# Spectral filter and state-space mix: the time transform's real and imaginary parts on two halves of the partitions, and the filter's sums inside the inverse matmuls

## The chip, the cores and the metric

The kernel runs on one core of a Trainium2 chip. The metric is the device time of one launch in microseconds (us). Before the change it is 349.39 us, the median of three runs (348.5 to 349.62).

## What is computed

The input x has 2048 time steps of 1024 channels. Two branches read it, and a gate mixes them row by row.

```python
g = sigmoid((x * gate_w).sum(-1, keepdims=True))

X = rfft2(x)                        # over time (2048) and channels (1024 -> 513)
a = irfft2(X * (w_r + 1j * w_i))    # the spectral branch, w of 2048 x 513

Lam_bar = exp(exp(log_dt) * (Lambda_re + 1j * Lambda_im))
Bu = x @ (((Lam_bar - 1) / Lam)[:, None] * (B_re + 1j * B_im)).T
h[t] = Lam_bar * h[t - 1] + Bu[t]   # the state-space branch, 1024 complex states
b = 2 * (h @ (C_re + 1j * C_im).T).real + x * Dskip

out = g * a + (1 - g) * b
```

## The kernel before

Everything is bf16 in SBUF and fp32 in PSUM. The kernel body records operations, each with an engine, a key and an assumed duration; the class Plan (L99 to L221) then orders them, engine by engine: among the operations that its own clock holds ready first, the one with the lowest key goes next. The order on every engine, SyncE's (SP's) queue of DMA issues included, is thus fixed before the launch, and a queue waits at its head. The constants K_... (L820 to L836) set the keys.

**State-space branch.** The 1024 states are eight blocks (jb), each done in two turns of 1024 time steps. `bu` multiplies x by B (64 matmuls a block, L743), ScalarE copies the sums out (L746), VectorE rotates them by a cosine and sine table (`rot`, L711 to L717), scans them (L755) and rotates them back (`rot_out`). Three buffers u hold turns between the matmuls and the scans. `load_BT` (L727) brings B by a transposing DMA on SP, two for a block; `load_CT` (L695) brings C in eight transposing DMAs, each behind a step of the last spectral stage.

**Spectral branch.** The time index of 2048 is split in 128 times 16. The stages are:

- `fd` (L511) and `s1` (L526), 16 steps j: the channel transform, then the 128-point time transform as a complex product, four matmuls of 512 columns (L530 to L533) with the tables T2 and TK. The result, real and imaginary parts side by side in the columns, goes to DRAM (L538).
- `s2w` (L618), 16 steps b, which starts when all of `s1` is in DRAM: it loads a tile Bb across (L620), and the 16 rows b of w_r and w_i (L622, L623, 128 KB each) into the tile wA. Four matmuls with block diagonal cosines and sines (L627 to L630) do the second step of the time transform. ScalarE copies out X2 (L633). VectorE makes the complex product with w: two multiplications of 1024 columns, by w_r and by w_i with the halves swapped (L637, L638), and a difference and a sum of 512 columns (L639, L640), the result X3 in wB. wA has two places for w, wB four for X3.
- The channels 0 and 512 share a column and need a repair: `fixup` (L585) turns that column through DRAM, and GpSimd computes it (L603 to L612) into Qb; ScalarE puts it into column 0 of each X3 (L641).
- `is1` (L643): the 128-point inverse, again four matmuls (L648 to L651), the copy C1 (L654), and a store to DRAM (L655).
- `is2` (L660) and `idft` (L677), 16 steps bp, which start when all of `is1` is in DRAM: a load Cq (L662), 8 small matmuls, a copy ZT (L673), the inverse channel transform, the gate (L690) and a store to DRAM (L691). After the even steps a `load_CT` follows.

**Output.** `yout` (L779), 16 tiles of 128 rows, each 32 matmuls of 512 columns with C (L787), eight small ones for Dskip (L794) and VectorE's sums with the loaded spectral part. Its first tile waits for `idft` step 13, all others for step 15 (the item "step", L790).

**Memory.** Large tiles take one of four places of 16 KB a partition (group "b8") in the order in which they are declared: bn, T2_sb, TK_sb, wA, wB, then the four CT. Bb, X2 and C1 lie in the upper half of the last state buffer; the scans of the blocks 6 and 7 wait until the last of them is read (the item "lodged", L759).

Of the kernel before, what the change touches and what calls it, by code (L numbers as in the profile page):

```python
# [11 lines left out]
ACT = mybir.ActivationFunctionType  # L12
# [23 lines left out]
def _host_consts():  # L36
# [14 lines left out]
    for par in range(2):  # L51
# [19 lines left out]
    c4 = np.kron(np.cos(2 * np.pi * (np.outer(np.arange(16), np.arange(16)) % 16) / 16), np.eye(4))  # L71
    s4 = np.kron(np.sin(2 * np.pi * (np.outer(np.arange(16), np.arange(16)) % 16) / 16), np.eye(4))
    R4 = np.block([[c4, s4], [-s4, c4]])
# [8 lines left out]
        T2=bf(np.stack([Tc, Ts], axis=2)),  # L82
        TK=bf(np.concatenate([-Ts, np.stack([Kc, Ks, -Ks, J, P0], axis=1)], axis=1)),
        R4=bf(R4),
# [144 lines left out]
def kernel(  # L229
# [27 lines left out]
    turn2_dram = dram.tile([2, 16, P, K], BF16, name="turn2_scratch")  # L257
# [57 lines left out]
    vec8 = cpool.tile([8, 5, P], BF16, name="vec8")  # L315
    for i, src in enumerate((B_Lambda_re, B_Lambda_im, B_log_dt, gate_w, B_Dskip)):
        dma(0, 0.05, lambda i=i, src=src: nc.scalar.dma_start(out=vec8[:, i, :], in_=src.rearrange("(j p) -> j p", p=P)),
            w=[("vec8", i)], eng="ACT", issue=0.33)
# [12 lines left out]
    T2_sb = tile_of([P, 16, 2, P], BF16, "T2_sb", "b8")  # L331
    TK_sb = tile_of([P, 21, P], BF16, "TK_sb", "b8")
    R4_sb = cpool.tile([P, P], BF16, name="R4_sb")
    dma(16.1, 2.6, lambda: nc.sync.dma_start(out=G_all, in_=cst["G"].rearrange("p d k -> p (d k)")), w=[("G",)])
    dma(16.2, 2.6, lambda: nc.sync.dma_start(out=T2_sb.t, in_=cst["T2"]), w=[(T2_sb,)])
    dma(16.3, 1.7, lambda: nc.sync.dma_start(out=TK_sb.t, in_=cst["TK"]), w=[(TK_sb,)])
    dma(16.4, 0.2, lambda: nc.sync.dma_start(out=R4_sb, in_=cst["R4"]), w=[("R4",)])
    T2 = lambda j, c: T2_sb.t[:, j, c, :]
    Tn = lambda j: TK_sb.t[:, j, :]
    Kc, Ks, Kns, JJ, J0 = [lambda i=i: TK_sb.t[:, 16 + i, :] for i in range(5)]  # L340
# [47 lines left out]
    def f():  # L388
        for i in range(5):
            nc.tensor.transpose(out=vps.t[:, i, :], in_=vec8[:, i, :], identity=ident[0:8, 0:8])  # L390
    pe(0.5, 0.2, f, r=[("vec8", i) for i in range(5)] + [("ident",)], w=[(vps,)])
# [134 lines left out]
    def s1(j, X1, key):  # L526
        psa = psum([P, 2, K], "ps_s1")

        def f():
            mm(psa.t[:, 0, :], lhsT=T2(j, 0), rhs=X1.t[:, 0, :], start=True, stop=False)  # L530
            mm(psa.t[:, 0, :], lhsT=T2(j, 1), rhs=X1.t[:, 1, :], start=False, stop=True)
            mm(psa.t[:, 1, :], lhsT=T2(j, 0), rhs=X1.t[:, 1, :], start=True, stop=False)
            mm(psa.t[:, 1, :], lhsT=Tn(j), rhs=X1.t[:, 0, :], start=False, stop=True)  # L533
        pe(key, 4 * U, f, r=[(X1,), (T2_sb,), (TK_sb,)], w=[(psa,)])
        A1 = tile_of([P, 2, K], BF16, "A1", "A1")
        act(key, 1.01, lambda: nc.scalar.copy(out=A1.t, in_=psa.t), r=[(psa,)], w=[(A1,)])  # L536
        act(key, 0.2, lambda: nc.scalar.copy(out=Acol[:, j, :], in_=A1.t[:, :, 0]), r=[(A1,)], w=[("Acol", j)])
        dma(key, 0.68, lambda: nc.sync.dma_start(out=turn1_dram[j], in_=A1.t), r=[(A1,)], w=[("t1", j)])  # L538

    Wr_v = A_w_r.rearrange("(p b) k -> p b k", b=16)  # L540
    Wi_v = A_w_i.rearrange("(p b) k -> p b k", b=16)
    Wc, Wc_f, Wh, alpha, beta = [fx.tile([P, 16, n], d, name=m) for n, d, m in (
        (4, BF16, "Wc"), (4, FP32, "Wc_f"), (4, FP32, "Wh"), (2, FP32, "alpha"), (2, FP32, "beta"))]
    Wrev, Zrev = fx.tile([P, 16, 4], FP32, name="Wrev"), fx.tile([P, 16, 2], FP32, name="Zrev")
    Bcol, Qb, Zp = [fx.tile([P, 16, 2], BF16, name=m) for m in ("Bcol", "Qb", "Zp")]
    Zp_f, t1, t2, t3, t4 = [fx.tile([P, 16, 2], FP32, name=m) for m in ("Zp_f", "q1", "q2", "q3", "q4")]
    al2, be2 = [fx.tile([P, 16, 2, 2], FP32, name=m) for m in ("al2", "be2")]
# [8 lines left out]
    def reverse_m(src, ncol, name, dst, item, ditem, key):  # L556
        rps = psum([P, 16, ncol], name + "_ps")

        def f():
            for b in range(16):  # L560
                if b == 0:
                    mm(rps.t[:, 0, :], lhsT=J0(), rhs=src[:, 0, :], start=True, stop=True)
                else:
                    mm(rps.t[:, b, :], lhsT=JJ(), rhs=src[:, 16 - b, :], start=True, stop=True)
        pe(key, 1.0, f, r=item + [(TK_sb,)], w=[(rps,)])
# [19 lines left out]
    def fixup(key):  # L585
# [3 lines left out]
        def f():  # L589
            with nc.allow_non_contiguous_dma(reason="tiny corner turn"):  # L590
                nc.sync.dma_start(out=Bcol, in_=col0_dram.rearrange("(a b) j c -> j a b c", a=8))
        dma(key, 0.6, f, r=[("col0",)], w=[("Bcol",)])
        zps = psum([P, 2, 16], "zps")

        def f():
            mm(zps.t[:, 0, :], lhsT=Kc(), rhs=Bcol[:, :, 0], start=True, stop=False)
            mm(zps.t[:, 0, :], lhsT=Ks(), rhs=Bcol[:, :, 1], start=False, stop=True)
            mm(zps.t[:, 1, :], lhsT=Kc(), rhs=Bcol[:, :, 1], start=True, stop=False)
            mm(zps.t[:, 1, :], lhsT=Kns(), rhs=Bcol[:, :, 0], start=False, stop=True)
        pe(key, 0.5, f, r=[("Bcol",), (TK_sb,)], w=[(zps,)])  # L600
# [5 lines left out]
        pool(key, 0.8, lambda: G_.tensor_mul(out=t1, in0=Zp_f, in1=al2[:, :, 0, :]), r=[("Zp_f",)] + fa, w=[("t1",)])  # L606
        pool(key, 0.8, lambda: G_.tensor_mul(out=t2, in0=Zp_f[:, :, ::-1], in1=al2[:, :, 1, :]), r=[("Zp_f",)] + fa, w=[("t2",)])
        gp(lambda: G_.tensor_add(out=t1, in0=t1, in1=t2), ["t1", "t2"], ["t1"])
        pool(key, 0.8, lambda: G_.tensor_mul(out=t3, in0=Zrev, in1=be2[:, :, 0, :]), r=[("Zrev",)] + fb, w=[("t3",)])
        pool(key, 0.8, lambda: G_.tensor_mul(out=t4, in0=Zrev[:, :, ::-1], in1=be2[:, :, 1, :]), r=[("Zrev",)] + fb, w=[("t4",)])  # L610
        gp(lambda: G_.tensor_add(out=t3, in0=t3, in1=t4), ["t3", "t4"], ["t3"])
        gp(lambda: G_.tensor_add(out=Qb, in0=t1, in1=t3), ["t1", "t3"], ["Qb"])  # L612

    t1_v = turn1_dram.rearrange("j (a b) c k -> b (j a) c k", a=8)
    wA = tile_of([P, 4, 2, K], BF16, "wA", "b8")
    wB = tile_of([P, 4, 2, K], BF16, "wB", "b8")

    def s2w(b, key):  # L618
        Bb = tile_of([P, 2, K], BF16, "Bb", "Bb")
        dma(key - 6, 0.84, lambda: nc.sync.dma_start(out=Bb.t, in_=t1_v[b]), r=[("t1", j) for j in range(16)], w=[(Bb,)])  # L620
        wr, w1, w2 = (wA, "W", b % 2), (wA, "a"), (wA, "b")
        dma(key - 6, 0.43, lambda: nc.sync.dma_start(out=wA.t[:, b % 2, 0, :], in_=Wr_v[:, b, 0:K]), w=[wr + (0,)])  # L622
        dma(key - 6, 0.43, lambda: nc.sync.dma_start(out=wA.t[:, b % 2, 1, :], in_=Wi_v[:, b, 0:K]), w=[wr + (1,)])  # L623
        ps2 = psum([P, 2, K], "ps_s2")

        def f():
            mm(ps2.t[:, 0, :], lhsT=Kc(), rhs=Bb.t[:, 0, :], start=True, stop=False)  # L627
            mm(ps2.t[:, 0, :], lhsT=Ks(), rhs=Bb.t[:, 1, :], start=False, stop=True)
            mm(ps2.t[:, 1, :], lhsT=Kc(), rhs=Bb.t[:, 1, :], start=True, stop=False)
            mm(ps2.t[:, 1, :], lhsT=Kns(), rhs=Bb.t[:, 0, :], start=False, stop=True)  # L630
        pe(key, 4 * U, f, r=[(Bb,), (TK_sb,)], w=[(ps2,)])
        X2 = tile_of([P, 2, K], BF16, "X2", "X2")
        act(key, 1.01, lambda: nc.scalar.copy(out=X2.t, in_=ps2.t), r=[(ps2,)], w=[(X2,)])  # L633
        Wb = lambda i: wA.t[:, b % 2, i:i + 1, :].to_broadcast([P, 2, K])
        wa, wb, X3 = lambda: wA.t[:, 2], lambda: wA.t[:, 3], lambda: wB.t[:, b % 4]
        x3 = (wB, b % 4)
        dve(key, 0.69, lambda: nc.vector.tensor_mul(out=wa(), in0=X2.t, in1=Wb(0)), r=[(X2,), wr + (0,)], w=[w1])  # L637
        dve(key, 0.69, lambda: nc.vector.tensor_mul(out=wb(), in0=X2.t[:, ::-1, :], in1=Wb(1)), r=[(X2,), wr + (1,)], w=[w2])  # L638
        dve(key, 0.42, lambda: nc.vector.tensor_sub(out=X3()[:, 0, :], in0=wa()[:, 0, :], in1=wb()[:, 0, :]), r=[w1, w2], w=[x3 + (0,)])  # L639
        dve(key, 0.42, lambda: nc.vector.tensor_add(out=X3()[:, 1, :], in0=wa()[:, 1, :], in1=wb()[:, 1, :]), r=[w1, w2], w=[x3 + (1,)])  # L640
        act(key + 1, 0.2, lambda: nc.scalar.copy(out=X3()[:, :, 0], in_=Qb[:, b, :]), r=[("Qb",)], w=[x3 + (0,), x3 + (1,)])  # L641

    def is1(b, key):  # L643
        X3, x3 = lambda c: wB.t[:, b % 4, c, :], (wB, b % 4)
        psc = psum([P, 2, K], "ps_is1")

        def f():
            mm(psc.t[:, 0, :], lhsT=T2(b, 0), rhs=X3(0), start=True, stop=False)  # L648
            mm(psc.t[:, 0, :], lhsT=Tn(b), rhs=X3(1), start=False, stop=True)
            mm(psc.t[:, 1, :], lhsT=T2(b, 0), rhs=X3(1), start=True, stop=False)  # L650
            mm(psc.t[:, 1, :], lhsT=T2(b, 1), rhs=X3(0), start=False, stop=True)  # L651
        pe(key, 4 * U, f, r=[x3 + (0,), x3 + (1,), (T2_sb,), (TK_sb,)], w=[(psc,)])
        C1 = tile_of([P, 2, K], BF16, "C1", "C1")
        act(key, 1.01, lambda: nc.scalar.copy(out=C1.t, in_=psc.t), r=[(psc,)], w=[(C1,)])  # L654
        dma(key, 0.86, lambda: nc.sync.dma_start(out=turn2_dram[:, b].rearrange("c u k -> u c k"), in_=C1.t), r=[(C1,)], w=[("t2", b)])  # L655

    t2_v = turn2_dram.rearrange("c b (a g i) k -> i (c b a) g k", a=4, g=2)
    ga_v = ga_dram.rearrange("(p b) n -> p b n", b=16)

    def is2(bp, key):  # L660
# [4 lines left out]
        def f():  # L665
            for kc in range(4):
                par, half = divmod(kc, 2)
                for gg in range(2):
                    mm(psz.t[:, kc, gg, :], lhsT=Cq.t[:, gg, 256 * half + par:256 * (half + 1):2],
                       rhs=R4_sb, start=True, stop=True)  # L670
        pe(key, 0.65, f, r=[(Cq,), ("R4",)], w=[(psz,)])
# [153 lines left out]
    K_TAB = 3.38  # L825
    K_F0 = 21.64
    K_F = 1.92
    K_W0 = 56.28
    K_W = 1.73
    K_WI = 1.83  # L830
    K_I0 = 14.79
    K_I = 8.12
# [91 lines left out]
```

## Time and profile before

The profiled execution has a span of 348.1 us, the median of the plain runs is 349.39 us; the rest lies around the span.

| part of the span (us) | what runs, besides `bu`, its scans and rotations | PE | DVE | ACT |
|---|---|---|---|---|
| 0 to 28 | x loaded and transposed, its halves | 85% | 66% | 72% |
| 28 to 103 | `fd`, `s1` | 99% | 97% | 96% |
| 103 to 124 | the turn through DRAM, first `s2w`, the repair of column 0 | 88% | 97% | 71% |
| 124 to 164 | `s2w`, `is1` | 98% | 96% | 76% |
| 164 to 178 | last `is1`, the turn through DRAM | 99% | 100% | 70% |
| 178 to 228 | `is2`, `idft`, loads of C | 98% | 100% | 91% |
| 228 to 344 | `yout` | 99% | 76% | 1% |

The shares are busy time over the length of the part. Over the whole span PE (TensorE's matmuls) is busy for 333.3 us, DVE (VectorE) for 303.4, ACT (ScalarE) for 193.6 and POOL (GpSimd) for 21.0. A busy share is a mean; what sets the time of a stage is to be read from what it waits for, and from what has no room left in it. The profile counts a matmul of 512 columns as 379 ns, but successive ones start 0.216 us apart.

### The profile page before, as it was taken

What the parts mean: (1) busy time and instruction counts of PE and PEld (TensorE: products, weight loads), DVE (VectorE), ACT (ScalarE), POOL (GpSimd) and SP (SyncE); (2) the same over time, 40 slices, a digit from 0 to 9 for tenths busy, and PEclk for the clock granted to TensorE, in tenths of its full rate; (3) what the DMA queues carried; (4) which work ended last, traced back from release to release, by engine and by line L of the source; (5) the groups of instructions that cost most, each with busy time, mean ns of one, the idle gap of its engine ahead of it and who ended that gap; (6) DMA issues with size and microseconds to landing.
All of it is one profiled execution on the core that took longest, in us unless ns stands there. A gap on an engine that the chain in (4) does not pass through costs nothing. (4 is left out here: it accounts for less than half of the span.)

```text
span 348.1 us, 5201 instructions
## 1 busy us (share of the span) xinstructions
PE 333.3 (96%) x1909; PEld 175.9 (51%) x1945; DVE 303.4 (87%) x508; ACT 193.6 (56%) x269; POOL 21.0 (6%) x47
## 2 busy tenths in 40 slices
PE   5999999999998999999999999999999999999994
PEld 4655554555543444444447566554544544544442
DVE  2969999899999998999999999999999999942321
ACT  3897999999996776876689999720000000000000
POOL 1180000000004700000000000000000000000000
PEclk9999999999999999999999999999999999999999
DMA  7999310431165789879279999952122222300001
GB/s 246 314 324 123 108 61 32 93 87 66 60 167 109 241 170 322 235 165 222 73 185 229 253 280 258 239 194 83 60 93 99 82 62 90 119 33 30 33 35 55
DMA packets 64433, 49.89 MB, mean 143 GB/s; under 512 B 38932, under 2 KB 51476, under 8 KB 64152
## 3 DMA queue, kind: packets, MB, share of 16 engines
q1 hardware_dynamic: 64136, 49.53, 53.5%
q8 instruction: 15, 0.25, 0.3%
q0 software_dynamic: 192, 0.02, 0.3%
q14 instruction: 10, 0.08, 0.1%
q10 hardware_dynamic: 80, 0.01, 0.0%
HBM read 24.89 MB, written 16.79 MB: 120 GB/s over the span
## 5 line engine op out<-in xcount | busy, mean ns | idle before, releaser
L743 PE MATMUL psu<-xT,BTs 128*128 128x512 bf16 x496 | 115.8, 379 | 1.2 <-DVE xT L365 0.2
L787 PE MATMUL ps_y<-CT,h 128*128 128x512 bf16 x499 | 111.9, 379 | 0.7
L743 PEld LDWEIGHTS <-BTs 128*128 128x128 bf16 x512 | 49.6, 98 | 57.0 <-issue 0.5
L787 PEld LDWEIGHTS <-h 128*128 128x128 bf16 x512 | 49.4, 98 | 56.4 <-DVE h L715 0.2
L755 DVE TENSOR_TENSOR_SCAN h<-r_sb,carry,u 128x512 bf16<-128x512 f32 x48 | 59.6, 1272 | 0.1
L814 DVE SCALAR_TENSOR_TENSOR o<-ps_y,omg,ga 128x1024 bf16<-128x1024 f32 (+1 forms) x17 | 21.0, 1240 | 27.5 <-PE ps_y L794 27.5
L746 ACT CAST u<-psu 128x1024 bf16<-128x1024 f32 x32 | 32.3, 1020 | 12.1 <-PE psu L743 11.9
L517 PE MATMUL ps_fd<-G_all,xpm 128*128 128x512 bf16 x125 | 29.9, 379 | 0.7 <-ACT A L536 0.5
L517 PEld LDWEIGHTS <-xpm 128*128 128x128 bf16 x128 | 18.5, 145 | 10.5 <-issue 0.8
L522 ACT CAST X<-ps_fd 128x1024 bf16<-128x1024 f32 x16 | 21.3, 1334 | 0.1
L711 DVE TENSOR_TENSOR su<-h,pn 128x1024 bf16<-128x1024 bf16 (+1 forms) x24 | 21.1, 878 | 0.1
L712 DVE TENSOR_TENSOR h<-h,pn 128x1024 bf16<-128x1024 bf16 (+1 forms) x24 | 21.0, 876 | 0.1
L711 DVE TENSOR_TENSOR su<-u,cs 128x2048 bf16<-128x2048 bf16 x16 | 19.4, 1215 | 0.3
L712 DVE TENSOR_TENSOR u<-u,cs 128x2048 bf16<-128x2048 bf16 x16 | 19.5, 1220 | 0.1
L755 DVE TENSOR_TENSOR_SCAN h<-r_sb,u 128x512 bf16<-128x512 f32 x16 | 19.2, 1219 | 0.0
L654 ACT CAST h<-ps_is 128x1024 bf16<-128x1024 f32 x16 | 16.2, 1016 | 4.8 <-PE ps_is L651 2.8
L633 ACT CAST h<-ps_s 128x1024 bf16<-128x1024 f32 x16 | 16.1, 1016 | 3.4 <-PE ps_s L630 2.1
L536 ACT CAST A<-ps_s 128x1024 bf16<-128x1024 f32 x16 | 16.5, 1030 | 0.0
L360 PE MATMUL pt<-ident,xn 128*128 128x128 bf16 x128 | 9.9, 242 | 4.0 <-DMA xn<-in_A_x_dram 3.9
L690 ACT ACTIVATE eo<-ps_id,gA 128x1024 bf16<-128x1024 f32 x11 | 12.4, 1168 | 1.9 <-PE ps_id L685 1.9
L673 ACT CAST ZT<-ps_is 128x1024 bf16<-128x1024 f32 x13 | 13.1, 1044 | 0.0
L713 DVE TENSOR_TENSOR h<-h,su 128x512 bf16<-128x512 bf16 (+1 forms) x24 | 12.6, 524 | 0.1
(166 smaller groups left out, 429.1 us busy)
## 6 DMA issues: line engine op xcount, KB each, us to landing
xn<-in_A_x_dram SPq DMA_DIRECT2D x16, 256.0 KB, 5.6
turn_scratch<-A SPq DMA_DIRECT2D x16, 256.0 KB, 2.0
h<-turn_scratch SPq DMA_DIRECT2D x16, 256.0 KB, 3.9
turn_scratch<-h SPq DMA_DIRECT2D x16, 256.0 KB, 4.2
out_dram<-o SPq DMA_DIRECT2D x15, 256.0 KB, 2.2
eoc<-ga_scratch SPq DMA_DIRECT2D x12, 256.0 KB, 2.8
Cq<-turn_scratch SPq DMA_DIRECT2D x11, 256.0 KB, 4.4
ga_scratch<-eo SPq DMA_DIRECT2D x11, 256.0 KB, 2.9
```

Of the source, the lines that this page charges most:

```text
L517: mm(pf.t[:, par].rearrange("p c k -> p (c k)"), lhsT=xA[:, par, db, j, :], rhs=G_sb[:, db, par, :], start=(db == 0), stop=(db == 3))
L522: act(key, 1.3, lambda: nc.scalar.copy(out=X1.t.rearrange("p c (k r) -> p r c k", r=2), in_=pf.t), r=[(pf, 0), (pf, 1)], w=[(X1,)])
L536: act(key, 1.01, lambda: nc.scalar.copy(out=A1.t, in_=psa.t), r=[(psa,)], w=[(A1,)])
L633: act(key, 1.01, lambda: nc.scalar.copy(out=X2.t, in_=ps2.t), r=[(ps2,)], w=[(X2,)])
L654: act(key, 1.01, lambda: nc.scalar.copy(out=C1.t, in_=psc.t), r=[(psc,)], w=[(C1,)])
L711: dve(key, w, lambda: nc.vector.tensor_mul(out=sv(), in0=src()[:, ::-1], in1=bc(1)), r=sitem + [titem(1)], w=[(su,)])
L712: dve(key, w, lambda: nc.vector.tensor_mul(out=dst(), in0=src(), in1=bc(0)), r=sitem + [titem(0)], w=ditem)
L743: mm(psu.t[:, ri, :], lhsT=BT.t[:, ri, db, :], rhs=xT[c][:, db, :], start=(db == 0), stop=(db == 7))
L746: act(kb[cc], 1.01, lambda cc=cc, psu=psu: nc.scalar.copy(out=u.t[:, :, cc, :], in_=psu.t), r=[(psu, 0), (psu, 1)], w=ui(cc))
L755: dve(kd, 1.25, lambda cc=cc, ri=ri, carry=carry: nc.vector.tensor_tensor_scan(out=g()[:, ri, cc, :], data0=rb, data1=u.t[:, ri, cc, :], i ...
L787: mm(psy.t[:, 512 * dh:512 * (dh + 1)], lhsT=hbuf[jb // 4].t[:, jb % 4, ri, P * tb:P * (tb + 1)], rhs=CT[pc].t[:, ri, jb % 2, 512 * dh:512 ...
L814: dve(key - 1, 0.2 + 1.07e-3 * (b - a), lambda a=a, b=b: nc.vector.scalar_tensor_tensor(out=o.t[:, a:b], in0=psy.t[:, a:b], scalar=og, in1 ...
```

## The change

1. **Halves of the partitions.** `s1` now makes, for each parity h of the frequency index, real parts on partitions 0 to 63 and imaginary parts on 64 to 127. It still has four matmuls of 512 columns; their tables are overlapping slices of TF.
2. **Second step in one pass.** `s2w` multiplies the whole tile by one matrix RF: two matmuls for four.
3. **The filter.** X2 is multiplied by w_r and by w_i, each in place over its copy of w (Z(b, 0) and Z(b, 1)). The difference and the sum are gone; `is1` adds the two products in PSUM, with four matmuls as before, whose tables are overlapping slices of MI.
4. **Loads of w.** Both halves of the partitions need the same w, so four DMAs load it (two tensors, two halves, 128 KB each) where two did. wA and wB together now hold w and the products of four steps b; w of step b + 4 is loaded when `is1` of step b has been read.
5. **The repair.** A memset on GpSimd clears column 0 of Z(b, 1). The repaired column goes through four more small matmuls (qps) and a copy (Qz) before ScalarE puts it into Z(b, 0). Its small tensors share memory with others, and GpSimd's first product waits for all eight factors. Bcol is loaded in two DMAs.
6. **Tables.** T2 and TK (1024 and 672 KB) become TF (two tiles of 768 KB) and a small TK. MI (two tiles of 768 KB) is loaded into the places that TF leaves: the second one after the last `s1`.
7. **Keys.** K_TAB, K_W0, K_WI and K_I get other values.

```diff
+    TF_sb = [tile_of([P, 8, 2, 192], BF16, "TF_sb", "b8") for _ in range(2)]
+    TK_sb = cpool.tile([P, 9, P], BF16, name="TK_sb")
+    for i in range(2):
+        dma(16.2, 2.0, lambda i=i: nc.sync.dma_start(out=TF_sb[i].t, in_=cst["TF"][:, 8 * i:8 * (i + 1)]), w=[(TF_sb[i],)])
+    dma(16.3, 1.0, lambda: nc.sync.dma_start(out=TK_sb, in_=cst["TK"]), w=[("TK",)])
...
         def f():
-            mm(psa.t[:, 0, :], lhsT=T2(j, 0), rhs=X1.t[:, 0, :], start=True, stop=False)
-            mm(psa.t[:, 0, :], lhsT=T2(j, 1), rhs=X1.t[:, 1, :], start=False, stop=True)
-            mm(psa.t[:, 1, :], lhsT=T2(j, 0), rhs=X1.t[:, 1, :], start=True, stop=False)
-            mm(psa.t[:, 1, :], lhsT=Tn(j), rhs=X1.t[:, 0, :], start=False, stop=True)
+            tf = TF_sb[j // 8].t
+            for h in range(2):
+                mm(psa.t[:, h, :], lhsT=tf[:, j % 8, h, 64:192], rhs=X1.t[:, 0, :], start=True, stop=False)
+                mm(psa.t[:, h, :], lhsT=tf[:, j % 8, h, 0:128], rhs=X1.t[:, 1, :], start=False, stop=True)
...
+        qps = psum([P, 2, 16], "qps")
+        def f():
+            for odd in range(2):
+                for c in range(2):
+                    mm(qps.t[64 * c:64 * (c + 1), odd, :], lhsT=SEL(odd, c), rhs=Qb[:, :, c], start=True, stop=True)
+        pe(key, 0.3, f, r=[("Qb",), ("TK",)], w=[(qps,)])
+        act(key, 0.2, lambda: nc.scalar.copy(out=Qz, in_=qps.t), r=[(qps,)], w=[("Qz",)])
...
+    MI_sb = [tile_of([P, 16, 192], BF16, "MI_sb", "b8") for _ in range(2)]
+    for i in range(2):
+        dma(30 + 16 * i, 2.0, lambda i=i: nc.sync.dma_start(out=MI_sb[i].t, in_=cst["MI"][:, 16 * i:16 * (i + 1)]), w=[(MI_sb[i],)])
+    home = lambda b: (wA, wB)[b // 2 % 2]
+    Z = lambda b, i: home(b).t[:, 2 * (b % 2) + i]
 
     def s2w(b, key):
         Bb = tile_of([P, 2, K], BF16, "Bb", "Bb")
         dma(key - 6, 0.84, lambda: nc.sync.dma_start(out=Bb.t, in_=t1_v[b]), r=[("t1", j) for j in range(16)], w=[(Bb,)])
-        dma(key - 6, 0.43, lambda: nc.sync.dma_start(out=wA.t[:, b % 2, 0, :], in_=Wr_v[:, b, 0:K]), w=[wr + (0,)])
-        dma(key - 6, 0.43, lambda: nc.sync.dma_start(out=wA.t[:, b % 2, 1, :], in_=Wi_v[:, b, 0:K]), w=[wr + (1,)])
+        wr = (home(b), b % 2)
+        for i in range(2):
+            for c in range(2):
+                dma(key - 6, 0.5, lambda i=i, c=c: nc.sync.dma_start(out=Z(b, i)[64 * c:64 * (c + 1)], in_=W_v[i][b][:, :, 0:K]), w=[wr + (i, c)])
+        pool(key - 4, 0.1, lambda: nc.gpsimd.memset(Z(b, 1)[:, :, 0:1], 0.0), w=[wr + (1, 0), wr + (1, 1)])
...
-            mm(ps2.t[:, 0, :], lhsT=Kc(), rhs=Bb.t[:, 0, :], start=True, stop=False)
-            mm(ps2.t[:, 0, :], lhsT=Ks(), rhs=Bb.t[:, 1, :], start=False, stop=True)
-            mm(ps2.t[:, 1, :], lhsT=Kc(), rhs=Bb.t[:, 1, :], start=True, stop=False)
-            mm(ps2.t[:, 1, :], lhsT=Kns(), rhs=Bb.t[:, 0, :], start=False, stop=True)
+            for h in range(2):
+                mm(ps2.t[:, h, :], lhsT=RF, rhs=Bb.t[:, h, :], start=True, stop=True)
...
-        dve(key, 0.69, lambda: nc.vector.tensor_mul(out=wa(), in0=X2.t, in1=Wb(0)), r=[(X2,), wr + (0,)], w=[w1])
-        dve(key, 0.69, lambda: nc.vector.tensor_mul(out=wb(), in0=X2.t[:, ::-1, :], in1=Wb(1)), r=[(X2,), wr + (1,)], w=[w2])
-        dve(key, 0.42, lambda: nc.vector.tensor_sub(out=X3()[:, 0, :], in0=wa()[:, 0, :], in1=wb()[:, 0, :]), r=[w1, w2], w=[x3 + (0,)])
-        dve(key, 0.42, lambda: nc.vector.tensor_add(out=X3()[:, 1, :], in0=wa()[:, 1, :], in1=wb()[:, 1, :]), r=[w1, w2], w=[x3 + (1,)])
+        for i in range(2):
+            dve(key, 0.69, lambda i=i: nc.vector.tensor_mul(out=Z(b, i), in0=X2.t, in1=Z(b, i)),
+                r=[(X2,)], w=[wr + (i, 0), wr + (i, 1)])
...
     def is1(b, key):
...
+            for h in range(2):
+                at = lambda lo: MI_sb[b // 8].t[:, 2 * (b % 8) + h, lo:lo + P]
+                mm(psc.t[:, h, :], lhsT=at(0), rhs=Z(b, 0)[:, h, :], start=True, stop=False)
+                mm(psc.t[:, h, :], lhsT=at(64), rhs=Z(b, 1)[:, h, :], start=False, stop=True)
...
-    K_TAB = 3.38
+    K_TAB = 4.93
-    K_W0 = 56.28
+    K_W0 = 56.75
-    K_WI = 1.83
+    K_WI = 1.97
-    K_I = 8.12
+    K_I = 10.67
```

## The prediction

> **What bounds the kernel now.** I read the totals first, then the busy time by stage, then the DMAs that two stages issue, then SP's order of issues.
>
> ```profile
> span 348.1 us, 5201 instructions
> PE 333.3 (96%) x1909; PEld 175.9 (51%) x1945; DVE 303.4 (87%) x508; ACT 193.6 (56%) x269; POOL 21.0 (6%) x47
> ```
>
> TensorE is busy for nearly all of the span, and so is VectorE until the last 50 us. By this view alone, work taken from TensorE comes straight off the time. The view by stage has the length, then the busy us of PE, PEld, DVE, ACT and POOL, the clock, the DMA share and GB/s:
>
> ```profile
> 112.00:124.00 12.00, 10.87 (x67) 4.99 (x68) 11.43 (x18) 8.29 (x13) 7.97 (x15) 1.00 0.71 213
> 124.00:164.00 40.00, 39.14 (x178) 17.53 (x180) 38.43 (x69) 30.38 (x44) 0.00 (x0) 1.00 0.91 225
> 164.00:178.00 14.00, 13.89 (x65) 6.34 (x66) 13.98 (x22) 9.75 (x16) 0.00 (x0) 1.00 0.36 114
> 178.00:228.00 50.00, 48.98 (x377) 31.76 (x382) 49.97 (x72) 45.69 (x58) 0.00 (x0) 1.00 1.04 248
> ```
>
> The reader is to see the last column but one. From 124 to 164, where `s2w` and `is1` run, the DMA engines are 0.91 busy, and from 178 to 228 (`is2`, `idft`) 1.04: they have no room left there. So three things are full at once, and the DMAs decide what a change in this stretch is worth. The DMAs issued in these two stages (count, size, median us to landing; the first four rows from 124 to 164, the last two from 178 to 228):
>
> ```profile
> turn_scratch<-h SPq DMA_DIRECT2D x13, 256.0 KB, 4.4
> h<-turn_scratch SPq DMA_DIRECT2D x8, 256.0 KB, 3.9
> wA<-in_A_w_r_dram SPq DMA_DIRECT2D x11, 128.0 KB
> wA<-in_A_w_i_dram SPq DMA_DIRECT2D x11, 128.0 KB, 3.5
> ...
> Cq<-turn_scratch SPq DMA_DIRECT2D x11, 256.0 KB, 4.4
> ga_scratch<-eo SPq DMA_DIRECT2D x9, 256.0 KB, 2.9
> ```
>
> The stages are a chain: `yout` needs `idft` step 15 (L790), `idft` needs all of `is1` in DRAM, `s2w` all of `s1`. From 228 on TensorE runs `yout` back to back (114.95 us busy of 116), so a later start of `yout` is a later end, one for one.
>
> **What one DMA costs.** Two equations, in engine time. From 124 to 164: 0.91 x 40 = 36.4 us for 32 plain loads and stores of 256 KB (13 + 8 + 22 halves) and 4 transposing loads of B of 256 KB. From 178 to 228: 52 us for 29 plain ones (15 Cq, 14 eo) and 17 transposing units (8 loads of C of 512 KB, one of B). They give 0.96 us for a plain 256 KB and 1.42 us for a transposing one. A load of w (128 KB) thus costs 0.48 us.
>
> **The change, part by part.**
>
> TensorE. `s2w` loses 2 of 4 matmuls in 16 steps, 32 in all. In the timeline successive ones of a step start at 124.62, 124.84, 125.05 and 125.27: 0.216 us each, so 6.9 us are gone. `s1` and `is1` keep their 64. The four matmuls of qps are of the kind of L596 to L599, which start 0.03 us apart: nothing.
>
> VectorE. L639 and L640 go: 32 instructions whose mean is 0.422 and 0.428 us, 13.6 us. The two products stay: one of 1024 columns takes 0.682 and 0.688 us with its broadcast or swapped operand (L637, L638), and plain ones of that size take 0.690 (L711, `rot_out`). VectorE is not what ends last after 296, so this only keeps it from being late.
>
> Loads of w. 64 instead of 32, of the same 128 KB. Before, 4 go out at 20 us, 6 from 114 to 123, 22 from 127.85 to 162.2. After, wA and wB hold w for four steps, so 16 go out early, around 20 to 28 us, where the queue is full (0.98 busy from 0 to 28) but the next load on it, of B at 29.37, is for block 2, turns later. The other 48 all wait for `is1` of four steps before; the first `is1` runs at 122.90 now. So the stretch from then on has 48 loads for 22: 48 x 0.48 - 22 x 0.48 = **+12.5 us** of DMA time. No trace row has a load onto half of the partitions. Bounds: 0.37 us, from the best slice of the stage (132 to 134: 370 GB/s at a share of 1.05, so 352 GB/s full), and 0.96, if a load on half the partitions ran at half the rate. The nearest row is the load of w itself, same bytes and same rows of 1 KB, so I take 0.48.
>
> The Trainium skill, page "SBUF — State Buffer", section "Door 1: The DMA port swizzle (why `[64,N]` ≈ `[32,N]`)", says that partitions 0 to 63 reach only 8 of 16 DMA ports, and gives 196 GB/s for them against 328 for all 128. By it a load would be 0.48 x 328 / 196 = 0.80 us (an estimate), and the sum below 21.8 us instead of 6.5. No row of this trace shows it.
>
> SP's queue. The 26 more issues take 0.33 to 0.53 us each, some 11 us, where SP now has issues worth about 23 us in the 40: room, but it waits at its head, and a load of w that waits for `is1` holds the Bb and the stores of C1 behind it.
>
> Tables. MI's second half (768 KB, three units, 2.9 us) goes out at about 103, after the last matmul of `s1`, ahead of the last store of A (issued at 104.3) that the first Bb waits for. From 104 to 108 the engines are 0.35 busy, so 0 to 2.9 us of delay. The repair gets qps and a copy (0.2 us, as L566), up to 1 us before the first `is1`. Together I take **+1 us**, bounds 0 and 3.9. The first half of MI, TF and the small TK move where the share is 0.39 (28 to 103): nothing, and 2.4 us if that room were gone. The memsets on POOL (a MEMSET has 0.10 us) lie between landing and product: hidden while w lands steps ahead, some 0.2 us a step, 3 us in all, if not.
>
> Room that takes it up. From 124 to 164 the engines have 0.09 x 40 = **3.6 us** free. From the last load of w (162.2) to the first Cq (issued at 176.8) 14.6 us pass, of which the chain needs 3.5 (landing) + 1.4 (products) + 0.2 (column) + 0.9 (`is1`) + 1.0 (copy) + 4.2 (store landing) = 11.2; `bu` takes the rest of the slots. So **3.4 us** more.
>
> Sum: 12.5 + 1 - 3.6 - 3.4 = **+6.5 us** for the start of `yout`. The 6.9 us saved on TensorE are then idle time: `bu` runs further ahead in `s2w` (VectorE has 13.6 us more for it) and is missing later, between 178 and 235. The span becomes 354.6 us. The plain median is 1.3 above the profiled span, so **355.9 us**. With a load at 0.37 the sum is 7.2 + 1 - 7 = +1.2 (350.6); at 0.64, a third of the way to the upper bound, it is 30.7 - 10.6 + 1 - 7 = +14.2, so I end this case at 364.
>
> **Rivals.**
>
> *The engines decide (faster).* For it: TensorE has 98% and VectorE 96% in the stretch; the waits named there are small (L637 and L638 waited for w for 0.8 and 0.7 us in all, and ACT 1.6 for a store), so the DMAs only just keep up and do not clearly lead; prefetch four steps deep may fill the queue better than two. Then all of TensorE's 6.9 us come off: 349.39 - 6.9 = 342.5. Against it: the shares of 0.91 and 1.04. If half of the DMA time added is hidden it is some 345.
>
> *It cancels out (same).* `yout` starts at 228 as before, since added traffic just fills the 7 us of room, and the matmuls saved are idle: 349.4.
>
> *Half the partitions, half the rate (much slower).* At 0.96 the 48 loads take 46.1 us: 35.5 + 1 - 7 = +29.5, 379. At 0.72, two loads on opposite halves overlapping partly, 24 + 1 - 7 = +18, 367. For it nothing in this trace; against it, consecutive loads alternate between the halves and can run side by side. The skill's page would have it near 371.
>
> *The loads of w wait for the ring.* Each place is free only after `is1`; its turn is 1.7 (four issues) + 3.5 + 0.2 + 1.4 + 0.2 + 0.9, about 8 us for four steps, against some 16 that the DMAs take. It does not decide, and has its weight in the first case.
>
> **How the numbers follow.** A difference of 0.3%, 1 us, is what a measurement of this kernel tells from none. DMA-paced slower: 0.48. Half rate: 0.10. Same: 0.10. Engines decide: 0.32. The likeliest is 355.9, its own range 350.5 to 364. For 8 in 10 I reach down to 342.5, which takes in most of the faster case, and up to 366, which leaves out most of the half rate. Faster 0.32, same 0.10, slower 0.58.
>
> **What would show it.** Right: DMA share near 1 from about 125 until the first Cq, loads of w landing in over 4 us, the first Cq at about 183 and the first long run of ps_y at about 234 instead of 227.55, with 10 us or more of PE idle before that, and PE still back to back after it; `s2w` with 32 matmuls and DVE near 290 us. Wrong: the first Cq before 177 with PE above 97% from 124 to 228; then the engines set the pace and the time is near 342. Wrong upwards: loads of w that cost over 0.6 us each in a stretch where little else is moved.

## The result, and the profile after

The changed kernel takes 353.17 us (median of 9 runs, 352.50 to 354.36), against 349.69 us (9 runs, 348.5 to 352.5) for the kernel before on the same chip: a ratio of 1.0093, 95% interval 1.0066 to 1.0119. It is slower, by 3.5 us. In this document a time is the median of all executions, while a ratio leaves out those more than 1.5% above the fastest of their kernel (one each of e2, f1, f3, h1 and h2). The profiled span grows from 348.1 to 350.7 us. First the totals of the kernel after, then its busy time by stage (length; busy us of PE, PEld, DVE, ACT, POOL; clock; DMA share; GB/s):

```profile
span 350.7 us, 5296 instructions
PE 331.2 (94%) x1917; PEld 172.9 (49%) x1917; DVE 293.7 (84%) x476; ACT 193.5 (55%) x270; POOL 21.9 (6%) x63
```

```profile
112.00:124.00 12.00, 8.25 (x48) 3.27 (x48) 9.38 (x14) 7.38 (x12) 7.74 (x16) 0.86 0.71 198
124.00:164.00 40.00, 36.04 (x167) 15.87 (x166) 34.39 (x49) 30.54 (x47) 0.97 (x9) 1.00 0.91 233
164.00:178.00 14.00, 12.46 (x58) 5.49 (x57) 12.55 (x19) 10.67 (x16) 0.32 (x3) 1.00 1.04 229
178.00:228.00 50.00, 48.55 (x367) 30.27 (x365) 49.90 (x70) 42.05 (x52) 0.00 (x0) 1.00 0.96 238
```

VectorE's total falls by 9.7 us. From 112 to 178 TensorE is idle for 9.3 us, where it was idle for 2.1 before, and the DMA share from 164 to 178 goes from 0.36 to 1.04. Times of some events (start us, from the timelines of both kernels) show where the 2.6 us of the span come from:

| event | before | after | later by |
|---|---|---|---|
| last store of A issued | 104.3 | 104.5 | 0.2 |
| first Bb issued | 108.5 | 111.5 | 3.0 |
| first `is1` on TensorE | 122.9 | 126.8 | 3.9 |
| last load of w issued | 162.2 | 174.3 | 12.1 |
| first Cq issued | 176.8 | 184.7 | 7.9 |
| first long run of ps_y | 227.55 | 231.05 | 3.5 |
| end | 348.1 | 350.7 | 2.6 |

So the first `is1` loses 3.9 us, the stretch of the loads of w another 8.2, the tail to the first Cq gives back 4.2, the C stage (first Cq to `yout`) 4.4 and the rest 0.9.

The line that was not foreseen is SP's own timeline. This is the beginning of the stretch in the kernel after (start, us, line, operation, tile, how many):

```profile
127.65 1.30 SPq L659 DMA_DIRECT2D wA<-in_A_w_r_dram  x2
129.06 1.24 SPq L659 DMA_DIRECT2D wA<-in_A_w_i_dram  x2
130.39 0.55 SPq L686 DMA_DIRECT2D turn_scratch<-h  x1
131.04 1.25 SPq L659 DMA_DIRECT2D wA<-in_A_w_r_dram  x2
132.39 1.24 SPq L659 DMA_DIRECT2D wA<-in_A_w_i_dram  x2
133.73 0.55 SPq L686 DMA_DIRECT2D turn_scratch<-h  x1
```

Each row ends some 0.1 us before the next begins, and so it goes on to 177: only two pauses between issues are longer than 0.15 us (0.22 and 0.45). Issue by issue, SP is busy from 127 to 177 for 28.9 us with 48 loads of w, 7.4 with stores of C1, 3.9 with transposing loads of B and 3.1 with Bb: 43.3 of 50, and the steps from one issue to the next take nearly all of the rest. In the kernel before, the issues in this window are 23.1 us, and pauses longer than 0.15 us are 24.5. What one issue of a load of w takes, in the kernel before and after (minimum, median and maximum in ns, first and last start):

```profile
L622 SPq DMA_DIRECT2D wA<-in_A_w_r_dram x16: 327/336/489, 20.2 to 161.6; - x16
```

```profile
L659 SPq DMA_DIRECT2D wA<-in_A_w_r_dram x16: 595/602/746, 20.3 to 163.6; - x16
```

The load has the same 128 KB, but it is cut into 64 partitions with two rows each instead of 128 with one, and SP is busy with it for 0.6 us instead of 0.34.

### The profile page after: what moved, and what is told of

The parts are those of the page before. It is cut to its first block, busy times and chain, and to the rows that moved or that the text cites. A ratio compares the mean times of both kernels' runs of the same rounds, so it can differ in the third digit from the quotient of the medians.

```text
span 350.7 us, 5296 instructions
## 1 busy us (share of the span) xinstructions
PE 331.2 (94%) x1917; PEld 172.9 (49%) x1917; DVE 293.7 (84%) x476; ACT 193.5 (55%) x270; POOL 21.9 (6%) x63
## 4 chain that ended last, share of the span: by engine, by line
PE 58%; DVE 16%; ACT 10%; DMA 9%; SPq 4%; issue 2%; DVEq 0%; POOL 0%; POOLq 0%; ACTq 0%
PE ps_y L818 32%; PE psu L774 13%; DVE h L786 5%; PE ps_id L716 3%; PE ps_fd L532 3%; DMA wB<-in_A_w_r_dram 3%; DMA xn<-in_A_x_dram 2%; PE ps_y L825 2%; DVE su L742 2%; ACT u L777 2%; PE pt L375 2%; SPq L659 2%; DMA h<-turn_scratch 1%; DVE wB L670 1%; ACT X L537 1%
## 5 line engine op out<-in xcount | busy, mean ns | idle before, releaser
L774 PE MATMUL psu<-xT,BTs 128*128 128x512 bf16 x512 | 117.0, 379 | 1.5 <-ACT h L685 1.2
L818 PE MATMUL ps_y<-CT,h 128*128 128x512 bf16 x512 | 113.7, 379 | 0.0
L670 DVE TENSOR_TENSOR wA<-h,wA 128x1024 bf16<-128x1024 bf16 x16 | 10.8, 695 | 7.2 <-ACT h L668 2.6
L721 ACT ACTIVATE eo<-ps_id,gA 128x1024 bf16<-128x1024 f32 x12 | 13.4, 1153 | 1.4 <-PE ps_id L716 1.4
L716 PE MATMUL ps_id<-G_all,ZT 128*128 128x256 bf16 x104 | 13.0, 273 | 1.0 <-ACT ZT L704 1.0
```

The source lines that it names most:

```text
L716: mm(pz.t[:, at, :], lhsT=ZT.t[:, 2 * par + half, c, :], rhs=Gi_sb[:, par, half, c, :], start=(half == 0), stop=(half == 1))
L774: mm(psu.t[:, ri, :], lhsT=BT.t[:, ri, db, :], rhs=xT[c][:, db, :], start=(db == 0), stop=(db == 7))
L818: mm(psy.t[:, 512 * dh:512 * (dh + 1)], lhsT=hbuf[jb // 4].t[:, jb % 4, ri, P * tb:P * (tb + 1)], rhs=CT[pc].t[:, ri, jb % 2, 512 * dh:512 ...
```

## The experiments

Theory at the outset: the loads of w set the pace from the first `is1` to the first Cq by their DMA time, now some 0.6 us each. Rivals: the order of work around the tables and the column repair; the engines. The kernels ran in four sets, and the kernel before had 349.69, 350.05, 349.68 and 350.68 us in them. The ratio is to the kernel before of the same set; the last column is from the profiled execution.

| kernel | us | ratio, 95% interval | first `is1` to first Cq, us |
|---|---|---|---|
| before | 349.69 | | 53.9 |
| after | 353.17 | 1.0093 (1.0066 to 1.0119) | 57.9 |
| e1, two loads | 347.51 | 0.9931 (0.9901 to 0.9960) | 38.5 |
| e2, four full loads | 346.45 | 0.9896 (0.9837 to 0.9955) | 52.5 |
| e3, MI late | 354.25 | 1.0122 (1.0071 to 1.0173) | 58.0 |
| e4, matmuls back | 358.05 | 1.0223 (1.0168 to 1.0278) | 60.3 |
| f1, interleaved | 351.25 | 1.0035 (0.9995 to 1.0076) | 56.2 |
| f3, interleaved, wide | 350.50 | 1.0013 (0.9976 to 1.0051) | 52.1 |
| e6, every second partition | 353.43 | 1.0117 (1.0044 to 1.0191) | 58.0 |
| e9, half from ACT | 375.03 | 1.0713 (1.0652 to 1.0774) | 63.7 |
| g1, joined rows | 351.30 | 1.0053 (1.0022 to 1.0084) | 56.0 |
| g2, joined, qps earlier | 353.36 | 1.0090 (1.0056 to 1.0124) | 55.1 |
| h1, half from GpSimd | 358.62 | 1.0182 (1.0124 to 1.0241) | 57.3 |
| h2, interleaved, half from GpSimd | 349.48 | 0.9967 (0.9932 to 1.0002) | 54.0 |

### Half of the loads taken away (e1)

```diff
         for i in range(2):
-            for c in range(2):
-                dma(key - 6, 0.5, lambda i=i, c=c: nc.sync.dma_start(out=Z(b, i)[64 * c:64 * (c + 1)], in_=W_v[i][b][:, :, 0:K]), w=[wr + (i, c)])
+            dma(key - 6, 0.5, lambda i=i: nc.sync.dma_start(out=Z(b, i)[:, 1, :], in_=(Wr_v, Wi_v)[i][:, b, 0:K]), w=[wr + (i, 0), wr + (i, 1)])
...
-            dve(key, 0.69, lambda i=i: nc.vector.tensor_mul(out=Z(b, i), in0=X2.t, in1=Z(b, i)),
+            dve(key, 0.69, lambda i=i: nc.vector.tensor_mul(out=Z(b, i), in0=X2.t, in1=Z(b, i)[:, 1:2, :].to_broadcast([P, 2, K])),
```

> Of each step's four loads of w onto 64 partitions two are left, each of 128 KB onto all 128 partitions, and both halves of the product read them: half of w is left out, other rows of it are used. Theory (the DMA time of the loads of w sets the pace from the first is1 to the first Cq): 24 loads for 48 in the stretch take about 12 us for 29, TensorE is full there again, its 6.9 us come off: 342.5 to 346 us, TensorE's idle time from 124 to 228 near nothing. Rival (the loads only fill room, the loss is in the order of work around the tables and the column repair): 352 to 354 us as before this edit.

Measured 347.51 us, 5.7 less than the changed kernel. The first Cq goes out at 167.3 instead of 184.7, and TensorE is busy for 38.58 of 40 us from 124 to 164. The loads are the cause of the loss. The time is 1.5 us above the range, though the first Cq is 17 us earlier: much of `bu` is then left for the C stage, which takes 59.7 us instead of 46.4, and before 124 TensorE lost time (8.18 us busy of 12 from 112 to 124, at a mean clock of 0.57; see the last section).

### Same bytes onto all partitions (e2)

```diff
-                dma(... out=Z(b, i)[64 * c:64 * (c + 1)], in_=W_v[i][b][:, :, 0:K] ...)
+                dma(... out=Z(b, i)[:, c, :], in_=(Wr_v, Wi_v)[i][:, b, 0:K] ...)
```

> Same number of loads of w and same bytes as in the changed kernel, but each goes onto all 128 partitions (one half of a place) instead of onto 64; other rows of w are used in the product. If the 64 partitions are what made a load cost 0.61 us instead of 0.48: 48 x 0.13 = 6 us of DMA time less in the stretch, 347 to 349 us, and loads alone in flight faster than 202 GB/s. If the bytes or the number of issues (SP issues one in 0.62 us) set the price: 352.5 to 354 us, and still one load each 0.6 us.

Measured 346.45 us, 0.55 below the range: 6.7 less than the changed kernel with the same bytes and the same number of loads, and 3.2 less than the kernel before. So neither the bytes nor the count, but the shape of the load costs the time. Two things changed with it at once: SP's issue (row below), and the rate (window from 128 to 164: 288 GB/s instead of 244).

```profile
L659 SPq DMA_DIRECT2D wA<-in_A_w_r_dram x16: 327/393/622, 20.0 to 156.3; - x16
```

### MI's place (e3) and the matmuls given back (e4)

```diff
-        dma(30 + 16 * i, 2.0, lambda i=i: nc.sync.dma_start(out=MI_sb[i].t, in_=cst["MI"][:, 16 * i:16 * (i + 1)]), w=[(MI_sb[i],)])
+        if i == 0:
+            dma(30, 2.0, lambda i=i: nc.sync.dma_start(out=MI_sb[i].t, in_=cst["MI"][:, 0:16]), w=[(MI_sb[i],)])
...
+    dma(60, 2.0, lambda: nc.sync.dma_start(out=MI_sb[1].t, in_=cst["MI"][:, 16:32]), r=[("t1", j) for j in range(16)], w=[(MI_sb[1],)])
     for b in range(3):
         s2w(b, KW(b))
```

> The second half of MI goes out after the last stores of A and the first loads of Bb instead of ahead of them. If its 2.9 us ahead of the store delay the first is1 one for one and the rest follows: 350 to 350.7 us, first is1 near 124. If the stretch behind is paced by DMA time in sum, the 768 KB are only moved into it: 352 to 353.2 us, with the first is1 earlier and the last load of w where it was.

Measured 354.25 us, above both ranges. The first Bb goes out at 108.9 again (the wait for A's store is 3.1 instead of 6.1 us), so MI was in its way as forecast. But Qb is ready at 121.0, as in the changed kernel (121.1), and the first `is1` still runs at 127.3: taking MI out of this place does not bring it forward. MI is not cleared by this altogether, since it now stands ahead of six loads of Bb, and TensorE waits 2.0 us for one of them (117.9 to 119.9).

```diff
-                mm(ps2.t[:, h, :], lhsT=RF, rhs=Bb.t[:, h, :], start=True, stop=True)
+                for _ in range(2):
+                    mm(ps2.t[:, h, :], lhsT=RF, rhs=Bb.t[:, h, :], start=True, stop=True)
-        pe(key, 2 * U, f, r=[(Bb,), ("TK",)], w=[(ps2,)])
+        pe(key, 4 * U, f, r=[(Bb,), ("TK",)], w=[(ps2,)])
```

> Both matmuls of each s2w are done twice, so TensorE has its 32 matmuls (6.9 us) back and all loads stay. Theory (DMA sets the pace, TensorE idles in the stretch): 353 to 354.7 us, its idle time before yout smaller by about 6. Rival (the engines set the pace): 359 to 360 us.

Measured 358.05 us, 4.9 more than the changed kernel: between both forecasts. The profiled execution was the quickest of the four (355.46 us). In it the loads of w go out over 47.0 us (46.7 in the changed kernel), and the first Cq at 184.7 as there, with 6.9 us of matmuls put in: so far the theory holds. The chain is 2.4 us longer because its first `is1` came earlier, at 124.4; TensorE's clock was not lowered in this run (see the last section). After the first Cq time is lost: the C stage takes 48.3 us instead of 46.4. The idle time of TensorE was thus not free. The matmuls of `bu` run in it, and what is not done there is done in the C stage, where TensorE has no room. The rows show the matmuls of `bu` between the first Cq and the long run of ps_y, in the kernels before, after and with the matmuls back (length; busy us of PE and ACT with `bu` alone, and how many; clock, DMA share and GB/s of the whole):

```profile
176.80:227.55 50.75, 27.47 (x116) 8.00 (x8) 1.00 1.05 249
184.66:231.05 46.39, 21.46 (x94) 7.22 (x7) 1.00 0.99 248
184.70:233.03 48.33, 23.90 (x103) 7.12 (x7) 1.00 1.01 243
```

At 0.216 us each, the 22 matmuls fewer are 4.8 us, for a stage that is 4.4 us shorter, and the 9 that come back are 1.9 us, for 1.9. (The records of the first and the third kernel lack some 16 of the 512 matmuls of `bu`.)

### Which of the two prices: issue or rate (f1, f3, e6, g1, e9)

These kernels take apart what e2 changed together. The first lays the tables out so that real and imaginary parts lie on partitions 2q and 2q + 1 (columns of RF, rows of MI, and the selection of the repaired column); each load then writes one row of w to two neighbours.

```diff
...
-            for c in range(2):
-                dma(... out=Z(b, i)[64 * c:64 * (c + 1)], in_=W_v[i][b][:, :, 0:K] ...)
+            for h in range(2):
+                dma(... out=Z(b, i)[:, h, :], in_=W_v[i][b][:, None, h, 0:K].to_broadcast([64, 2, K]) ...)
```

> The tables put real and imaginary parts on even and odd partitions (2q + c) instead of on the two halves, so that a load of w covers all 128 partitions: each row of w is written to two neighbouring partitions by one load, four loads of 128 KB a step as in the changed kernel; the whole function is computed. Theory (64 contiguous partitions made a load slow): as the run with four full loads, 345.5 to 347.5 us, loads issued every 0.43 to 0.47 us where they are alone, DMA share about 1.00 and 280 to 290 GB/s from 128 to 164. Rival (that run was quick because it read other rows of w, each once): 351 to 354 us.

> As the interleaved kernel, but two rows of w (1026 numbers) go in one piece, two loads of 256 KB a step instead of four of 128 KB. If the number of loads costs (an issue each on SP): 343 to 346 us. If only bytes and partitions count: as the interleaved kernel, 345.5 to 347.5. The places are 513 numbers apart, so VectorE's products may slow from 0.69 us; if they do, 347 to 352.

> Real and imaginary parts on even and odd partitions, and each load of w goes onto 64 partitions again: every second one of the 128. The whole function is computed. If it is where the 64 partitions lie (a contiguous half) that makes a load slow: 345.5 to 347.5 us and an issue every 0.45 us where loads are alone. If it is their number: 352 to 354.5 us and an issue every 0.62.

The interleaved kernel (f1) took 351.25 us, the rival's value (the profiled execution 354.13). Its DMAs are no longer full, and yet it gains only 1.9 us. The window from 128 to 164, and one step of SP's timeline:

```profile
128.00:164.00 36.00, 32.24 (x147) 14.21 (x148) 29.91 (x43) 27.73 (x44) 0.85 (x8) 1.00 0.80 241
```

```profile
134.01 1.20 SPq L658 DMA_DIRECT2D wA<-in_A_w_r_dram  x2
135.30 1.20 SPq L658 DMA_DIRECT2D wA<-in_A_w_i_dram  x2
136.59 0.55 SPq L685 DMA_DIRECT2D turn_scratch<-h  x1
137.23 1.20 SPq L658 DMA_DIRECT2D wB<-in_A_w_r_dram  x2
```

A fifth of the DMA time is free (from 132 to 168, after its first `is1` at 130.2, the share is 0.82), and SP is still issuing without a pause: a load takes it 0.56 us, the next one begins 0.65 us after it, and from 130 to 177 one pause is longer than 0.15 us (0.43). The rival's reason (rows read twice) is not it either: the DMAs have room, and the wide kernel below reads every row twice and is quicker in the stretch. SP's issuing is a pace by itself. Nor does SP only wait there for transfers ahead of it: a load issued after SP had paused for over a microsecond takes as long, 0.535 us in f1 (at 24.1, 26.1 and 30.0 us) and 0.595 in the changed kernel (at 25.5, 29.9 and 36.9).

In the wide kernel (f3), half as many loads of 0.53 to 0.58 us relieve SP, and the chain needs 52.1 us as in e2, with 326 GB/s from 128 to 164. Its products stay at 0.697 us. It loses in the C stage, where TensorE is busy for 45.44 of 50 us; 350.50 us is above the ranges for products that do not slow. Why its C stage (50.4 us) is longer than that of e2 (46.8), with as many matmuls of `bu` in it, stays open.

With every second partition (e6) the issues take 0.602 us and the time is 353.43, as in the changed kernel and as expected if the number of partitions counts. The Trainium skill, page "SBUF — State Buffer", section "Door 1: The DMA port swizzle (why `[64,N]` ≈ `[32,N]`)", would have such a load reach all 16 ports. SP was full in this run as well, so its time cannot show whether the ports were relieved; the DMA packets at the end of this section say a little of it.

```diff
-                dma(... out=Z(b, i)[64 * c:64 * (c + 1)], in_=W_v[i][b][:, :, 0:K] ...)
+                dma(... out=Zw(b, i)[64 * c:64 * (c + 1)], in_=W_2[i][b] ...)
```

> The changed kernel with its two halves and its four loads of w a step onto 64 partitions, in the same order on every queue; only each load reads its two rows of w per partition in one piece (1026 numbers, 64 pieces of 2 KB instead of 128 of 1 KB; the places of wA and wB are 513 numbers apart). New theory (what paces the stretch is SP, which takes 0.62 us to issue a load that is cut in two rows a partition, not the rate onto 64 partitions): issues of w drop to 0.32 to 0.45 us, SP is no longer busy from 128 to 176, 345.5 to 348.5 us. Rival (64 partitions, or the bytes, set the pace): issues still back up to 0.6 us, DMA share 0.95 or more, 352 to 354 us.

Measured 351.30 us: between both. Joining the two rows of a partition does not halve the issue. After a pause it takes 0.466 us instead of 0.595, so the second row costs a part, but back to back the medians are 0.55 to 0.59 us, and SP stays full. All kernels whose loads count 64 in the first dimension of the source (after, f1, f3, e6, g1) have medians of 0.55 to 0.61 us; those with 128 (before, e1, e2) 0.34 to 0.43. More than that the traces don't say.

> The changed kernel with the loads onto partitions 64 to 127 issued from ACT's queue, those onto 0 to 63 from SP's. If SP's 0.62 us an issue is the limit (the two halves could be written side by side): 346 to 349 us, and each landing in under 3.5 us. If the rate onto the partitions is the limit: 352 to 355 us, or later by what ACT loses to its 32 issues.

Measured 375.03 us, above both ranges. This run tells nothing of the limit: the early loads stood in ACT's queue until 43 us, and ACT's own work waited behind them (wait, us in total, times, longest):

```profile
ACT tt L502 <- DMA wA<-in_A_w_i_dram: 10.9, 1, 10.9
```

### A later step of the repair (g2)

```diff
-        gp = lambda fn, r, w, us=0.8: pool(key, us, fn, ...)
+        gp = lambda fn, r, w, us=0.5: pool(key, us, fn, ...)
...
```

> As the kernel with joined rows, and the scheduler is told 0.5 us instead of 0.8 for the seven GpSimd steps of the column repair, so that qps stands ahead of the last s2w step on TensorE instead of behind it. If the first is1 is late because qps waits in TensorE's order (Qb was ready 3.6 us before qps ran): first is1 some 1 us earlier, 0.5 to 1 us less than the joined kernel. If other work ends last: the same time as the joined kernel within 0.5 us.

Measured 353.36 us, 2.1 more than the joined kernel and outside both forecasts, with the first `is1` at 127.1: no gain. In the profiled executions qps came 3.3 us after Qb instead of 5.2, but Qb itself was ready at 121.0 instead of 119.6, and the scheduler had still put 16 matmuls of `bu` ahead of qps:

```profile
119.95 4.36 PE L776 MATMUL psu<-xT,BTs 128*128 128x512 bf16 x16
124.23 0.23 PE L639 MATMUL qps<-Qb,TK_sb 128*64 128x16 bf16 x4
```

Why the whole is 2.1 us longer is not shown. What a qps placed right behind Qb would bring was not tried.

### Both prices apart, and both gone (h1, h2)

Half of the loads go to GpSimd's queue; nothing else there waits for a load, since ACT's copy of the column now clears column 0 of Z(b, 1).

```diff
-        pool(key - 4, 0.1, lambda: nc.gpsimd.memset(Z(b, 1)[:, :, 0:1], 0.0), ...)
...
-                dma(... nc.sync.dma_start(...), w=[wr + (i, c)])
+                dma(... (nc.sync if c == 0 else nc.gpsimd).dma_start(...), w=[wr + (i, c)], eng="SP" if c == 0 else "POOL", ...)
```

> The changed kernel with the loads of w onto partitions 64 to 127 issued from GpSimd's queue, those onto 0 to 63 from SP's (and column 0 of the second product is zeroed by ACT's column copy instead of by a GpSimd memset, so that nothing on GpSimd waits for a load). SP loses 24 of its 48 issues of 0.62 us in the stretch, 15 us of 47.6. If SP's issuing is the pace and the DMAs have room behind it: 346 to 348.5 us, first Cq near 178. If the rate of loads onto 64 contiguous partitions is a pace of its own, nearly as slow: 351 to 353.5 us, DMA share near 1.00 with no more than 255 GB/s from 128 to 164.

> The interleaved kernel (loads onto all 128 partitions, real and imaginary part on neighbours) with half of the loads issued from GpSimd's queue, and the memset gone as in the other. If there are two paces, SP's issuing and the rate onto 64 partitions, this takes both away: 345.5 to 347.5 us, first Cq near 178, 280 GB/s or more from 128 to 164; faster than both kernels. If reading each row of w twice is what is slow: 350.5 to 353 us.

Measured 358.62 us (h1) and 349.48 us (h2). The profiled executions took 360.23 and 355.74 us, so only their stretch is read. Their first `is1` ran at 134.7 and 132.4; the windows from 136 to 172 of h1 and of h2:

```profile
136.00:172.00 36.00, 32.75 (x147) 14.32 (x149) 31.18 (x46) 30.08 (x43) 14.38 (x24) 1.00 1.10 265
```

```profile
136.00:172.00 36.00, 33.33 (x150) 14.69 (x151) 32.68 (x47) 30.70 (x43) 12.29 (x21) 1.00 1.00 318
```

In h1 SP's issues from 134 to 184 add up to 33.6 us, with 13.4 us of pauses, and the chain still needs 57.3 us: with 64 partitions the DMAs are full at 265 GB/s, and their share from 164 to 178 is 1.15. That is the second pace. The total of h1 is above both forecasts, and worse than the changed kernel's, for a reason outside the stretch: eight loads leave early from the second queue, the table G comes late, and TensorE waits for it (`ps_fd`, 4.8 us). In h2 both limits are eased (318 GB/s at a share of 1.00, 14.7 us of SP's pauses from 132 to 178), and the chain needs 54.0 us, as before the change; the total, 349.48 us, is the lowest of the kernels that compute the whole function with this change. It is 3.7 us under the changed kernel, and against the kernel before the interval (0.9932 to 1.0002) does not exclude equality. It carries the late start of h1 too: its last store of A is issued at 108.9 instead of 104.5. The forecast of 345.5 to 347.5 was missed by 2 us.

The rate by itself, GB/s over DMA share in the windows from 128 to 164: with loads onto 64 partitions 244 / 0.95 = 257 (after), 272 (e6), 266 (g1), 253 (h1); onto 128 partitions 288 (e2), 301 (f1), 323 (f3), 300 (h2). These windows hold other transfers too. From 36 to 43 us the only pieces of 1 KB (2 KB in g1 and f3) on the DMA engines are those of the loads of w; by the mean time of such a packet in the traces, a load of 128 KB takes the 16 engines 0.56 us in the changed kernel, 0.52 in g1 and 0.50 in e6, against 0.40 in e2, 0.41 in f1 and 0.35 in f3. So the load onto 64 partitions is dearer to the DMA engines too, by a factor of 1.4 from e2 to the changed kernel, and more than half of that stays when the 64 are spread over all 128 (e6).

## Why the prediction was right or wrong

**Sign and mechanism.** Slower, by a chain of DMAs from the first `is1` to the first Cq while TensorE idles: right, but for SP's part in it. e1 and e2 show it: without the added loads, or with loads of another shape, the time drops by 5.7 and 6.7 us. 355.9 was forecast, 353.17 measured; the start of `yout` is late by 3.5 us instead of 6.5. That the time came within 2.7 us is in part luck: the first `is1` was 2.9 us later than taken and the C stage 4.4 us shorter, and the plain median lies 2.5 us above the profiled span instead of 1.3.

**The loads of w, +12.5, and the room of 3.6.** Their sum of 8.9 us is near what the stretch lost (8.2), but by luck, for the price in it was mis-sized: 0.48 us a load was forecast, and after the change one costs 0.60 us of SP and about as much of the DMAs (from 38 to 42.6 us, where only these loads are in flight, the share is 0.94, with one issued each 0.62). With a price of 0.62 the added time is 48 x 0.62 - 22 x 0.48 = 19.2 us. Only 8.2 us came out because the stretch before had idle time to give: SP's pauses from 127 to 177 added up to 24.5 of 50 us in it.

**SP's queue.** This step failed: "The 26 more issues take 0.33 to 0.53 us each, some 11 us, ... room". They take 0.60, and SP has no room: from 127 to 177 its issues and the steps between them leave two pauses of 0.7 us in all. f1 shows it alone: DMA share 0.80, and 1.9 us gained. The Trainium skill, page "Perfetto Trace Analysis", section "What "DMA-bound" means", lists the issuing engine's sequencer, solid with DMA slices, as a way to be DMA-bound that is separate from the DMA engines. By that rule the row of SP is to be read like an engine's; the trace after agrees, with a load of w every 0.65 us.

**Half the partitions, half the rate.** The rival with 367 to 379 did not come, but it is partly true: the rate at a full share is 253 to 272 GB/s with these loads and 288 to 323 without, and the price is 0.6, not 0.96 or 0.80. The estimate of 0.80 from the Trainium skill's page was too high: by the packets the factor between 128 and 64 partitions is 1.4 (0.40 and 0.56 us), and its starting point of 0.48 was the mean of a mix.

**Tables and qps, +1 (0 to 3.9).** It is 3.9, the upper bound, for another reason than the one put first. The first Bb was 3.0 us late (111.5), but Qb only 0.8 us (121.1 for 120.3), and with MI out of the way of the first Bb (e3) the first `is1` came no earlier. The other 3.1 us lie behind Qb: qps runs at 124.74 and `is1` at 126.77, 5.7 us after Qb, where before it was 2.6 us; "up to 1 us before the first `is1`" took qps for a short step and left out the matmuls of `bu` that stand ahead of it in TensorE's order. That the order is the whole cause was not shown: in e4, where TensorE's clock stayed at 1.00 instead of 0.59 from 116 to 120, Qb was ready at 119.7 and the first `is1` ran at 124.4, with MI's load in the same place.

**The tail, -3.4.** It gave 4.2.

**"The 6.9 us saved on TensorE are then idle time."** This failed, and it is most of the distance between 355.9 and 353.17. With the same matmuls put back (e4) the time rises by 4.9 us. So some 4.9 of the 6.9 us were in use: `bu` ran in them, and the C stage, which has no room on TensorE, had 22 of its matmuls less to do and was 4.4 us shorter. The prediction let `bu` run ahead and then be "missing later", with no value for what was done already.

**The other rivals.** "The engines decide" falls with the first Cq, which e4 leaves at 184.7 with 6.9 us more matmuls; it holds only where the loads are gone (e1) or quick (e2). The loads hardly wait for their places: SP's issues of w wait for `is1` for 1.7 us in all from 127 to 177, so the ring did not decide.

**What would show it.** The DMA share near 1, loads landing in over 4 us (medians of 3.9 to 5.0 for 3.5), the first Cq at 183 (184.7) and DVE at 290 (293.7) came as stated. The long run of ps_y came at 231.05 instead of 234.

## What to carry to other kernels

A DMA has two prices, the time of the DMA engines and the time for which its queue is busy issuing it, and the second depends on how the transfer is cut up: read the queue's own timeline as one reads an engine's before more transfers are put on it. Idle time that appears on an engine in one stage is not lost work if a later, full stage has less to do for it; ask what runs in the gap. Before a tensor is laid out on half of the partitions, count the loads that then have to be doubled.

## What was not expected of the hardware

- A load of 128 KB took SP 0.33 to 0.43 us to issue onto 128 partitions from 128 rows, and 0.60 us onto 64 partitions with two rows each, from GpSimd's queue as well (0.60 in h1). The same row written to two neighbouring partitions took 0.54 to 0.56 us.
- A C1 store took 0.55 us to issue right behind such loads and 0.38 behind those of e2, though it is the same transfer; after a pause it took 0.36 to 0.38 us in all of them.
- TensorE's granted clock fell to half for several us behind short gaps in its work before the column repair, in the changed kernel and most of the others. In the joined kernel (g1) TensorE's longest gap there is 1.6 us (111.6 to 113.2), with one of 0.7 us behind it, and the clock (last column but two) is at half for the 6 us that follow:

```profile
112.00:114.00 2.00, 0.18 (x1) 0.11 (x2) 2.00 (x3) 0.48 (x1) 2.00 (x3) 1.00 0.92 87
114.00:116.00 2.00, 1.53 (x7) 0.35 (x7) 1.19 (x2) 1.64 (x3) 1.92 (x5) 0.50 0.89 293
116.00:118.00 2.00, 1.88 (x20) 0.69 (x18) 1.36 (x2) 1.34 (x3) 1.92 (x5) 0.50 1.00 353
118.00:120.00 2.00, 1.75 (x5) 0.60 (x6) 1.76 (x3) 2.00 (x4) 1.48 (x4) 0.50 0.82 279
```

In the changed kernel the clock is 0.59 from 116 to 120, and in the kernel before 1.00 from 112 to 124. The length of a gap alone does not decide it: in e4 gaps of 1.77 and 0.34 us (from 111.4 to 113.7), and in e3 one of 2.0 us, left the clock at 1.00. What the lower clock cost was not measured. The Trainium skill, page "TensorE: Matmul & The Clock Gate", section "HAM oscillation — how this bites in real kernels", puts the limit at idle gaps of some 3.4 us; here the clock fell behind gaps of 1.6 and 0.7 us.
